# Retention, MoE and SOLU-MoE on one core: the attention of the later pairs in chunks of 64, with the products of two token blocks' h between the turns

## The chip, the cores and the metric

One core of one Trainium2 chip runs the whole program. The metric is the device time of one execution in microseconds (us), lower is better. The kernel before takes 635.72 us, the median of 3 runs (634.75 to 636.51).

## What is computed

```python
def _attn_ref(q, k, v):                     # 4 batches, 8 heads, 576 positions, head_dim 64
    scores = scale * np.matmul(q, k.transpose(0, 1, 3, 2))
    gamma = 1.0 - 2.0 ** (-5.0 - np.arange(H))
    Dmat = np.where(rel >= 0, gamma[:, None, None] ** rel[None, :, :], 0.0)   # rel = query - key position
    return np.matmul(scores * Dmat[None], v)

def _moe_ref(x, w_in, w_out):               # 2304 tokens, 512 -> 2048 -> 512
    h = x @ w_in
    g = h * np.clip(h + 3.0, 0.0, 6.0) / 6.0
    return g @ w_out

def _moe2_ref(x, w_in, w_out, g_ln):        # 512 -> 1024 -> 512
    h = x @ w_in                            # then softmax times h, layer norm, times g_ln
    return ln @ w_out

def reference(...):
    x = attention output, heads side by side: (2304, 512)
    return _moe2_ref(_moe_ref(x, ...), ...)
```

## The kernel before, in words

The 32 heads are worked off as 16 pairs (two heads of one batch, one in partitions 0 to 63, one in 64 to 127). The attention has no softmax, so it runs in chunks: inside a chunk of 128 positions the scores are formed, masked and multiplied with v; what came before the chunk enters through a 64x64 state of each head. The 576 positions are four chunks of 128 and one of 64. For a pair `pr` there are:

- `load_pair` (line 908): four loads from memory on SP's queue, k and q transposed (`rk`, `rq`), k as rows (`rn`), v (`rv`). It is called three pairs ahead.
- `prep` (929): v scaled by the decay, on ScalarE or VectorE.
- `scores` (946): products of k and q into `s0`, `s1`; ScalarE copies them to `st` with a scale, GpSimd's affine select sets the part above the diagonal to zero.
- `short` (970): the last chunk's scores `z`, VectorE's mask of them, and the products of the old pair with its states into `xp`.
- `chunk_states` (1005): k times v for each chunk into `u`; VectorE forms the four running states with five instructions.
- `values` (1047): v times the masked scores into `xp`; then `evac_x` (1059): VectorE multiplies by a table (`tab_sb`), ScalarE and VectorE or GpSimd split the result into a rounded part and a rest (`x`), or SP stores it (`xd`).

A product in full fp32 is two matmul instructions with a weight load each; 64x64 tiles are four corners of the array. The MoE products run as three products of rounded and rest parts.

The loop at line 1096 goes over the pairs. Turn `pr` has the scores of pair `pr`, the states of pair `pr`, and what remains of pair `pr - 1`. From turn 5 on (`A_FROM`) one half of an h (`h_of`, line 650: 6 matmuls of 128x128x512, for token block 0 and the first six column groups of w_in, `FIRST`) is put behind each turn: 12 halves in 12 turns. After the loop, block 0's second product (`x2_units(0, FIRST)`, accumulators `acc`) alternates with block 1's h (line 1207), then come block 4's h, block 1's second product, and from line 1231 the `paired` stage, whose seven products per step (`sa` to `sd`) need sums of tokens (`early_forms`, `x_sums`) and sums of weights (`in_pair`).

What sets the order: the matmuls run in the order of the program text. All other work is put in order by a planner (class `Plan`, line 110), which gives each operation a due time from the matmuls behind it, and lets some vector work go to VectorE or GpSimd (`either`). Buffers of a tag are handed on in program order. The pools `ps_a` (accumulators of the attention) and `pa` (its buffers) are released before `ps_c` (accumulators `acc`) and `pb` (buffers of the later stages, among them `ws`, `wbo`, `wbi`, `g2`) are opened: an operation on a buffer of `pb` waits for all users of `pa`.

The weights come as 64-bit words and are put together on the core: a load into `wraw`, two ScalarE instructions (`wz`, `wt`), two VectorE ones, then the split (`words_of`): ScalarE, and VectorE or GpSimd. `out_later` (534) does this for six further groups of w_out, through two buffers `ws`, and `in_pair(3)` follows them in the order of `wraw`.

Of the kernel before, what the change touches and what calls it, by code (L numbers as in the profile page):

```python
# [24 lines left out]
FA = 6  # L25
GAMMA = [1.0 - 2.0 ** (-5 - h) for h in range(H)]
N_DEC = H + H // 2 + H // 2 + H // 2
NPAIR = NH // 2
NV = 5
BLOCKS = [(0, 512), (512, 512), (1024, 512), (1536, 512), (2048, 256)]  # L30
# [7 lines left out]
EARLY = 3  # L38
NE = 4
# [314 lines left out]
def retention_hardswish_solu_kernel(ctx, tc, kt, qt, kn, vt, w1, w2i, w2o, gln, decay, place, out):  # L354
# [70 lines left out]
    tab_sb = [pa.tile([128, S], F32, name=f"tab_sb{p}") for p in range(NP)]  # L425
# [3 lines left out]
    HEADS, ALL = [slice(0, 64), slice(64, 128)], slice(0, 128)  # L429
    CHUNKS = [slice(128 * c, min(128 * c + 128, S)) for c in range(NV)]  # L430

# [9 lines left out]
    for h in range(2):  # L441
        ge.affine_select(
            out=mask4[HEADS[h]], in_=mask4[HEADS[h]], compare_op=ALU.is_ge, fill=0.0,
            base=0, pattern=[[0, NP], [1, 64]], channel_multiplier=-1,
        )
# [40 lines left out]
    def raw_of(src):  # L486
        b = buf("wraw", [128, 512, 2], "wraw", I32)
        move(512, lambda: sy.dma_start(out=b().rearrange("p n t -> p (n t)"), in_=src), (), (b,))
        return b
# [406 lines left out]
    PA = {"rk": 3, "rq": 4, "rn": 3, "rv": 3, "v": 3, "st0": 2, "st1": 2, "state": 2, "st4": 2, "xa": 2}  # L896
# [4 lines left out]
    def pbuf(tag, shape, name):  # L901
        return pl.buf((ps_a, tag, 1), shape, F32, name)

    def at_x(c):

        return slice(128 + CHUNKS[c].start, 128 + CHUNKS[c].stop)

    def load_pair(pr):

        if pr >= NPAIR:  # L910
            return
        early = pr < EARLY
        tag = "wi" if pr < 2 else "g"
        rk, rq, rn, rv = (
            buf("g" if i == 3 else tag, shape, f"raw{pr}_{i}") if early else abuf(name, shape, f"{name}{pr}")
            for i, (name, shape) in enumerate((
                ("rk", [128, S]), ("rq", [128, S + 128]), ("rn", [128, 512]), ("rv", [128, 9, D]),
            ))
        )
        move(288, lambda: sy.dma_start(out=rk(), in_=kt[pr]), (), (rk,))  # L920
        n = S if early else S + 128
        move(n / 2, lambda: sy.dma_start(out=rq()[:, :n], in_=qt[pr][:, :n]), (), ((rq, 0),))
        move(288, lambda: sy.dma_start(out=rv(), in_=vt[pr]), (), (rv,))
        move(256, lambda: sy.dma_start(out=rn(), in_=kn[pr]), (), (rn,))
        if early:
            move(64, lambda: sy.dma_start(out=rq()[:, n:], in_=qt[pr][:, n:]), (), ((rq, 1),))
        raws[pr] = rk, rq, rn, rv

    def prep(pr):

        if pr >= NPAIR:
            return
        rv = raws[pr][3]
        v = vs[pr] = abuf("v", [128, 9, D], f"v{pr}")
        p = pr % NP
        for i, (c0, n, at) in enumerate(((0, 4, 2 * p), (4, 4, 2 * p + 1), (8, 1, H + NP + p))):
            def go(e, c0=c0, n=n, at=at):
                o, i = (x()[:, c0:c0 + n].rearrange("p c d -> p (c d)") for x in (v, rv))
                if e is se:
                    se.activation(out=o, in_=i, func=ACTF.Copy, scale=decay_sb[:, at:at + 1])  # L940
                else:
                    ve.tensor_scalar(out=o, in0=i, scalar1=decay_sb[:, at:at + 1], scalar2=None, op0=ALU.mult)

            either(0.3 if n > 1 else 0.15, 0.5 if n > 1 else 0.33, go, (rv,), ((v, i),), "ACT").earliest = 5.6

    def scores(pr):

        sp = [pbuf(f"s{h}", [128, 512], f"s{pr}_{h}") for h in range(2)]
        st = sts[pr] = [abuf(f"st{h}", [128, 512], f"st{pr}_{h}") for h in range(2)]
        k, q, _, _ = raws[pr]  # L950

        def go():
            for c in range(4):
                for o in range(2):
                    for h in range(2):
                        te.matmul(
                            sp[h]()[HEADS[o], CHUNKS[c]], k()[HEADS[h], 128 * c + 64 * o:128 * c + 64 * o + 64],
                            q()[HEADS[h], CHUNKS[c]], start=(c == 0), stop=(c == 3),
                        )

        pl.op("PE", 0.92, go, (k, (q, 0)), sp)
        for h in range(2):
            on_act(0.6, lambda h=h: se.activation(
                out=st[h](), in_=sp[h](), func=ACTF.Copy, scale=GAMMA[2 * (pr % NP) + h] ** -128), (sp[h],), (st[h],))
            on_ge(0.66, lambda h=h: ge.affine_select(
                out=st[h](), in_=st[h](), compare_op=ALU.is_ge, fill=0.0,
                base=0, pattern=[[0, 4], [1, 128]], channel_multiplier=-1,
            ), (st[h],), (st[h],))

    def short(pr, now, old):  # L970


        reads, writes = [], []
        if now:
            zp = pbuf("z", [128, 64], f"z{pr}")
            st4 = sts4[pr] = abuf("st4", [128, 64], f"st4{pr}")
            k, q, _, _ = raws[pr]
            reads, writes = [k, (q, 0)], [zp]
        if old:
            xp = xps[pr - 1] = pbuf("xp", [128, 1024], f"xp{pr - 1}")  # L980
            oq, v, state, ost4 = raws.pop(pr - 1)[1], vs[pr - 1], states.pop(pr - 1), sts4.pop(pr - 1)
            reads, writes = [*reads, oq, v, state, ost4], [*writes, xp]

        def go():
            for h in range(2):
                if old:
                    te.matmul(xp()[HEADS[h], at_x(4)], v()[HEADS[1 - h], 8], ost4()[HEADS[1 - h]], start=True, stop=False)
                if now:
                    te.matmul(zp()[HEADS[h]], k()[HEADS[h], CHUNKS[4]], q()[HEADS[h], CHUNKS[4]], start=True, stop=True)
            if not old:  # L990
                return
            rq, st = oq(), state()
            for c, w, qc in (
                (1, st[:, 0], rq[:, CHUNKS[1]]), (3, st[:, 2], rq[:, S:]),
                (2, st[:, 1], rq[:, CHUNKS[2]]), (4, st[:, 3], rq[:, CHUNKS[4]]),
            ):
                for h in range(2):
                    r = HEADS[h if c < 3 else 1 - h]
                    te.matmul(xp()[HEADS[h], at_x(c)], w[r], qc[r], start=(c == 1), stop=False)

        pl.op("PE", 0.24 * now + (0.45 if now else 0.6) * old, go, reads, writes)
        if now:
            on_ve(0.25, lambda: ve.tensor_tensor(out=st4(), in0=zp(), in1=mask4[:, pr % NP], op=ALU.mult), (zp,), (st4,))

    def chunk_states(pr):

        rn, v = raws[pr][2], vs[pr]
        up = pbuf("u", [128, 4, 64], f"u{pr}")
        state = states[pr] = abuf("state", [128, 4, 64], f"state{pr}")

        def go():
            kn_ = rn().rearrange("p (c d) -> p c d", d=128)
            for c in range(4):
                for h in range(2):
                    o = HEADS[1 - h if c == 3 else h]
                    te.matmul(up()[o, c], kn_[:, c, HEADS[h]], v()[:, 4 * h + c], start=(c == 0), stop=(c == 3))

        pl.op("PE", 0.52, go, (rn, v), (up,))

        def sums():  # L1020
            ve.tensor_copy(out=state()[:, 0], in_=up()[:, 0])
            for c, to, at in (
                (1, ((ALL, ALL),), H + pr % NP), (2, tuple(zip(HEADS, HEADS[::-1])), H + pr % NP),
                (3, ((ALL, ALL),), H + 2 * NP + pr % NP),
            ):
                for i, o in to:
                    ve.scalar_tensor_tensor(
                        out=state()[o, c], in0=state()[i, c - 1], scalar=decay_sb[i, at:at + 1], in1=up()[i, c],
                        op0=ALU.mult, op1=ALU.add,
                    )  # L1030

        on_ve(1.45, sums, (up,), (state,))

    def places():

        pp = bank("place", at=0)
        row = buf("r", [128, NP, 128], "place_sb")
# [51 lines left out]
    for pr in range(EARLY):  # L1089
        load_pair(pr)  # L1090
# [5 lines left out]
    for pr in range(NPAIR + 1):  # L1096
        more, past, joined = pr < NPAIR, pr > 0, pr > A_FROM
        if more:
            scores(pr)
# [15 lines left out]
    for _ in hs:  # L1115
        pass
# [518 lines left out]
```

## Time and profile before

| | |
|---|---|
| median of 3 runs | 635.72 us |
| profiled execution: time | 635.21 us |
| profiled execution: span of the trace | 633.5 us |
| granted TensorE clock over the span | 1.00 |
| TensorE (PE) busy | 622.9 us, 98% |
| VectorE (DVE) busy | 467.3 us, 74% |
| ScalarE (ACT) busy | 398.2 us, 63% |
| GpSimd (POOL) busy | 306.6 us, 48% |
| DMA | 145.99 MB, mean 230 GB/s |

PE is the matmul side of TensorE and PEld its weight loads, which overlap. Matmuls are pipelined, so the length of one (0.22 to 0.27 us for the small ones) says little; what an instruction costs is the distance between the starts of neighbours. "issue" as the end of a wait means that nothing that the profile shows was waited for. "q8 instruction" is the DMA queue that brings TensorE's program.

### The profile page before, as it was taken

The numbers are of one execution on the slowest core, as the hardware profiler recorded it, in microseconds if no ns is written. First come the engines' busy times: TensorE is split into PE (matmuls) and PEld (weight loads), VectorE is DVE, ScalarE is ACT, GpSimd is POOL, SyncE is SP. The second block draws the span as 40 slices with busy tenths as digits, with TensorE's granted clock in tenths as the row PEclk, the third lists the DMA queues.
The fourth block names the chain that finished last, engine by engine and source line by source line (L and its number), as shares of the span: only waits on it lengthen the run. The fifth ranks groups of instructions, "written<-read, shape, count | busy, mean of one in ns | idle before, by whom it ended". The sixth has DMA issues, their size and how long they took to land.

```text
span 633.5 us, 11326 instructions
## 1 busy us (share of the span) xinstructions
PE 622.9 (98%) x4095; PEld 519.3 (82%) x4095; DVE 467.3 (74%) x835; ACT 398.2 (63%) x687; POOL 306.6 (48%) x307
## 2 busy tenths in 40 slices
PE   7999999999999999999999999999999999999997
PEld 5788778889788888887888888888888888888887
DVE  4878899986778776789587787543687877878750
ACT  4778776874766561468476665421587777787582
POOL 6545553203144321533145230632379899999453
PEclk9999999999999999999999999999999999999999
DMA  9999997679756686645997669975585544344451
GB/s 326 381 347 380 398 328 255 252 233 310 242 190 230 224 301 242 228 161 192 360 345 271 223 224 386 391 255 187 153 237 116 114 90 113 101 84 101 83 106 61
DMA packets 92347, 145.99 MB, mean 230 GB/s; under 512 B 43906, under 2 KB 50178, under 8 KB 92292
## 3 DMA queue, kind: packets, MB, share of 16 engines
q1 hardware_dynamic: 92144, 145.26, 69.6%
q8 instruction: 32, 0.52, 0.3%
q14 instruction: 23, 0.19, 0.1%
q10 hardware_dynamic: 148, 0.02, 0.0%
HBM read 92.56 MB, written 43.25 MB: 214 GB/s over the span
## 4 chain that ended last, share of the span: by engine, by line
PE 81%; DMA 10%; DVE 5%; ACT 1%; issue 1%; SPq 1%; POOL 0%; DVEq 0%; POOLq 0%; ACTq 0%
PE acc L67 26%; PE h L67 20%; PE o L67 16%; PE sd L67 4%; PE sa L67 4%; PE sc L67 4%; DMA xd<-xa 4%; PE x L67 2%; PE sb L67 2%; PE xp L67 2%; DMA w1f_a<-w1w 2%; DMA w2s<-ws 1%; DMA wraw<-wf 1%; PE s L67 1%; DVE ws L67 1%
## 5 line engine op out<-in xcount | busy, mean ns | idle before, releaser
L67 PE MATMUL acc<-g,w1l 128*128 128x512 f32 x624 | 154.1, 389 | 0.0
L67 PEld LDWEIGHTS acc<-g,w1l 128*128 128x128 f32 x624 | 117.1, 188 | 24.4
L67 PE MATMUL o<-w,lt 128*128 128x512 f32 (+1 forms) x456 | 103.0, 378 | 0.0
L67 PEld LDWEIGHTS o<-w,lt 128*128 128x128 f32 x456 | 82.4, 188 | 16.3 <-POOL lt L67 0.4
L67 POOL TENSOR_TENSOR lt<-lT,lt 128x512 fp32r<-128x512 f32 x36 | 61.6, 1730 | 15.3 <-ACT lt L67 15.3
L67 ACT ACTIVATE e<-h,stat 128x1024 f32<-128x1024 f32 x36 | 41.3, 1148 | 35.7 <-DVE stat L67 35.4
L67 PE MATMUL h<-w2t,xt 128*128 128x512 f32 x216 | 53.5, 389 | 0.0
L67 PEld LDWEIGHTS h<-w2t,xt 128*128 128x128 f32 x216 | 40.3, 188 | 8.2
L67 PE MATMUL h<-x,w 128*128 128x512 f32 (+1 forms) x216 | 45.9, 361 | 0.0
L67 PE MATMUL acc<-g,w 128*128 128x512 f32 (+1 forms) x216 | 44.2, 355 | 1.4 <-DVE xa L67 0.9
L67 POOL TENSOR_TENSOR w1f_s<-ws,w1f_s 128x512 fp32r<-128x512 f32 x13 | 17.8, 1368 | 54.5 <-ACT w1f_s L67 54.5
L67 PEld LDWEIGHTS acc<-g,w 128*128 128x128 f32 x216 | 36.4, 189 | 8.5 <-ACT g L67 1.3
L67 PEld LDWEIGHTS h<-x,w 128*128 128x128 f32 x216 | 34.9, 189 | 7.1 <-issue 1.9
L67 PE MATMUL h<-w2b,xt 128*128 128x512 f32 x162 | 39.8, 390 | 0.0
L67 ACT ACTIVATE wz<-wraw 128x512 f32<-128x512 f32 x44 | 29.2, 669 | 14.2 <-DMA wraw<-in_w2o_dram 5.6
L67 DVE CUSTOM_DVE_ANT_0 wz<-wz,wt 128x1024 uint16<-128x1024 uint16 x44 | 36.1, 826 | 1.6 <-ACT wt L67 0.3
L67 ACT ACTIVATE wt<-wraw 128x512 int32<-128x512 uint32 x48 | 31.9, 665 | 8.2 <-DMA wraw<-in_w2o_dram 7.0
L67 DVE SCALAR_TENSOR_TENSOR h<-h,e 128x1024 f32<-128x1024 f32 x18 | 32.3, 1796 | 5.4 <-ACT e L67 5.3
L67 DVE TENSOR_SCALAR e<-h,stat 128x1024 f32<-128x1024 f32 x18 | 20.6, 1143 | 20.1 <-POOL stat L67 20.1
L67 PEld LDWEIGHTS h<-w2b,xt 128*128 128x128 f32 x162 | 30.2, 188 | 6.1
L67 DVE CUSTOM_DVE_ANT_0 h<-h,h 128x512 f32<-128x512 f32 x36 | 24.6, 683 | 12.9 <-ACT h L67 6.3
L67 POOL TENSOR_TENSOR xt<-x2r,xt 128x512 fp32r<-128x512 f32 (+1 forms) x18 | 23.9, 1346 | 19.2 <-ACT xt L67 19.2
(194 smaller groups left out, 1358.7 us busy)
## 6 DMA issues: line engine op xcount, KB each, us to landing
w1l<-w1s SPq DMA_DIRECT2D x34, 512.0 KB, 5.9
wraw<-in_w_dram SPq DMA_DIRECT2D x32, 512.0 KB, 5.9
w1s<-w1o SPq DMA_DIRECT2D x10, 512.0 KB, 3.3
x2l<-x2s SPq DMA_DIRECT2D x18, 256.0 KB, 6.7
x2f<-x2o SPq DMA_DIRECT2D x18, 256.0 KB, 3.9
x2r<-x2f SPq DMA_DIRECT2D x9, 512.0 KB, 4.3
rq<-in_qt_dram SPq DMA_DIRECT2D x13, 352.0 KB, 6.2
out_dram<-osb SPq DMA_DIRECT2D x17, 256.0 KB, 2.0
```

What stands on the lines that cost most here:

```text
L67: return lambda *args, **kw: self.keep(op(*args, **kw))
```

## The change

Pairs 0 to 4 (`LONG = 5`) stay in chunks of 128; their scores are now 64 rows by 128 columns of the array, half as many instructions, and the extra copy of q (`rqx`) is a load of its own. From pair 5 on the 576 positions are nine chunks of 64, every product is a 64x64 tile with 64 columns, and `attend(pr)` puts the products of pair `pr` (scores `s`, chunk products `u`) and of pair `pr - 1` (states `f`, values `y`) side by side, so that the four corners of the array work on four of them: 17 rounds of four products. VectorE now masks the scores straight from PSUM (`masked`), forms seven states with five instructions (ScalarE copies the first part), and multiplies by the table in two parts; the affine select is gone for these pairs.

The halves of h behind the turns are now those of block 0 and of block 1, 24 in all, handed out by a budget of 3.4 us per turn. Block 1's g lies in a tag of the pool `pa`. After the loop come block 1's second product, block 4's h, and block 0's second product, each without anything between.

```diff
+L, NC, C0 = 64, S // 64, 5
+LONG = 5
+FILL = 3.4
     def split_of(t, ff, name, src, r, tag="g", n=512):
-        w = GK[t, ff] = buf(tag, [128, 2, n], name, F32R)
+        w = GK[t, ff] = buf(tag, [128, 2, n], name, F32R) if tag else pl.buf((pa, "g", FA), WIDE, F32R, name)
     def h_of(t, ff, tag="g", extra=0.0):
-        hp = bank(f"h{t}_{ff}", n, None if t else 0)
+        hp = bank(f"h{t}_{ff}", n, None if t > 1 else 0)
-    PA = {"rk": 3, "rq": 4, "rn": 3, "rv": 3, "v": 3, "st0": 2, "st1": 2, "state": 2, "st4": 2, "xa": 2}
+    PA = {"rk": 3, "rq": 3, "rqx": 3, "rn": 3, "rv": 3, "v": 3, "st0": 2, "st1": 2, "state": 2, "xa": 3}
+    PARTS = (slice(0, C0), slice(C0, NC))
     # prep, from pair LONG on: one instruction over all nine chunks
+                either(0.42, 0.9, go, (rv,), ((v, i),))
+    def masked(pr, i, sp):
+        on_ve(0.1 + 0.067 * n, lambda: ve.scalar_tensor_tensor(
+            out=st(), in0=sp()[:, :n * L].rearrange("p (c q) -> p c q", q=L), scalar=decay_sb[:, at:at + 1],
+            in1=causal.unsqueeze(1).to_broadcast([128, n, L]), op0=ALU.mult, op1=ALU.mult), (sp,), (st,))
+    def state_of(pr, up):
+        on_act(0.4, lambda: se.activation(out=of(state())[:, 0], in_=us()[:, 0], func=ACTF.Copy), (up,), (state,))
+        def sums():
+            add(r[:, 1], r[:, 0], one, x[:, 1])
+            for c in range(1, 4):
+                add(r[:, 1, c], r[:, 1, c - 1], two, r[:, 1, c])
+            add(r[:, 0, 1:], r[:, 1, :3], one, x[:, 0, 1:])
+        on_ve(1.35, sums, (up, state), (state,))
+    def attend(pr):
+        now, old = pr if pr < NPAIR else None, pr - 1 if pr > LONG else None
...
+        def mm(b, c, left, right, swap, last=False):
+            for h in range(2):
+                o = HEADS[1 - h if swap else h]
+                te.matmul(b()[o, SHORT[c]], left(HEADS[h]), right(HEADS[h]), start=(b, h) not in begun, stop=last)
...
+        run([[(u, c), (y, c)] for c in range(5)], ...)
+        run([[(u, c), (f, c - 4)] for c in (5, 6, 7)], ...)
+            state_of(now, up)
+        run([[(s, 0), (f, 4)]], ...)
+            evac_x(old, 0, xp[0], xa)
+        run([[(s, c), (f, c + 4)] for c in (1, 2, 3, 4)], ...)
+            masked(now, 0, sp[0])
+        run([[(s, c), (y, c)] for c in (5, 6, 7, 8)], ...)
+            masked(now, 1, sp[1])
+            evac_x(old, 1, xp[1], xa)
+            split_x(old, xa)
+    def fillers():
+        for t, tag in ((0, "g"), (1, None)):
+            for ff in FIRST:
+                for i, _ in enumerate(h_of(t, ff, tag)):
+                    if i < 2:
+                        yield 1.36
     for pr in range(NPAIR + 1):
...
+        if pr < LONG:
+            long_scores(pr)
+            load_pair(pr + EARLY)
+            long_sums(pr)
+            prep(pr + 1)
+            long_rest(pr, pr - 1 if pr else None)
+        else:
+            if pr == LONG:
+                long_rest(None, pr - 1)
+            load_pair(pr + EARLY)
+            attend(pr)
+            prep(pr + 1)
         if pr >= A_FROM:
-            next(hs, None)
+            spent -= FILL
+            while spent < 0:
+                spent += next(fill, 9.0)
-    for i, _ in enumerate(x2_units(0, FIRST, evac_partial, ends=1)):
-        if i % NP == NP - 1:
-            for _ in h_of(1, FIRST[i // NP]):
-                pass
+    for _ in x2_units(1, FIRST, evac_partial):
+        pass
     for ff in FIRST:
         for _ in h_of(4, ff, next(slots_4)):
             pass
-    for _ in x2_units(1, FIRST, evac_partial):
+    for _ in x2_units(0, FIRST, evac_partial):
         pass
```

## Rows read from the trace of the kernel before

**Rows 1.** First part of the page and the clock line (engines; granted clock in tenths).

```profile
PE 622.9 (98%) x4095; PEld 519.3 (82%) x4095; DVE 467.3 (74%) x835; ACT 398.2 (63%) x687; POOL 306.6 (48%) x307
...
PEclk9999999999999999999999999999999999999999
```

**Rows 2.** Waits of PE, first 110 us: who, for whom; us, times, longest.

```profile
PE xp L67 <- issue: 2.3, 2, 1.4
...
PE acc L67 <- DVE xa L67: 0.9, 1, 0.9
```

**Rows 3.** Timeline of PE, one turn: start us, length us, instructions, form, count.

```profile
31.46 1.10 PE L67 MATMUL s<-rq,rk 64*64 64x128 f32 x32
32.38 0.22 PE L67 MATMUL z<-rq,rk 64*64 64x64 f32 x1
...
32.49 0.62 PE L67 MATMUL xp<-rq,state 64*64 64x128 f32 x16
33.04 0.69 PE L67 MATMUL u<-v,rn 128*64 128x64 f32 x16
33.56 1.05 PE L67 MATMUL xp<-st,v 128*64 128x128 f32 x16
34.53 1.65 PE L67 MATMUL h<-x,w 128*128 128x512 f32 x6
36.12 0.34 PE L67 MATMUL s<-rq,rk 64*64 64x128 f32 x4
```

**Rows 4.** Busy time by stretch: length; each engine's us (instructions); clock; DMA share, GB/s.

```profile
24.45:82.37 57.92, 55.71 (x1079) 44.62 (x1077) 46.45 (x115) 45.53 (x95) 33.41 (x38) 1.00 1.01 375
82.37:115.00 32.63, 32.62 (x142) 26.59 (x143) 30.96 (x41) 22.56 (x40) 13.78 (x8) 1.00 0.84 277
115.00:140.47 25.47, 25.47 (x147) 22.53 (x147) 22.52 (x46) 20.85 (x42) 1.98 (x2) 1.00 0.72 230
```

**Rows 5.** The same view between two stops of PE, and one later stretch.

```profile
15.82:21.52 5.70, 5.54 (x128) 4.68 (x128) 3.74 (x9) 3.50 (x10) 3.40 (x6) 1.00 1.05 393
...
34.53:41.50 6.97, 6.97 (x127) 5.54 (x129) 6.03 (x18) 5.68 (x13) 2.75 (x5) 1.00 0.99 334
```

**Rows 6.** Timeline of PE at two stops; in brackets the wait before.

```profile
15.82 0.33 PE L67 MATMUL xp<-raw,state 64*64 64x64 f32 x3 [1.38 <-issue]
...
28.25 0.65 PE L67 MATMUL xp<-rq,state 64*64 64x128 f32 x16 [0.90 <-issue]
```

**Rows 7.** DMA queues in 25.7-25.8, 29.9-30.1, 36.3-36.45 us: packets, MB, share.

```profile
q8 instruction: 1, 0.02, 69.2%
...
q8 instruction: 1, 0.02, 38.9%
...
q8 instruction: 1, 0.02, 45.8%
```

**Rows 8.** Groups of VectorE and GpSimd, 31.46 to 78.20 us: busy, mean ns.

```profile
L67 DVE TENSOR_TENSOR xa<-xp,tab_sb 128x576 f32<-128x576 f32 x10 | 7.5, 753 | 1.0 <-PE h L67 1.0
...
L67 DVE SCALAR_TENSOR_TENSOR state<-state,decay_sb,u 128x64 f32<-128x64 f32 x20 | 5.6, 281 | 0.7
...
L67 POOL TENSOR_SCALAR_AFFINE_SELECT st<-st 128x512 f32<-128x512 f32 x20 | 12.6, 654 | 17.4 <-ACT st L67 17.4
```

**Rows 9.** Groups of VectorE, 82.37 to 143 us.

```profile
L67 DVE TENSOR_TENSOR x_t<-xs_b,x_t 128x512 fp32r<-128x512 f32 x4 | 2.6, 677 | 0.0
...
L67 DVE SCALAR_TENSOR_TENSOR gf<-r,h 128x256 f32<-128x256 f32 x6 | 2.4, 412 | 0.1
...
L67 DVE TENSOR_TENSOR xs_b<-xs_b,xs_b 128x1024 f32<-128x1024 f32 x1 | 1.2, 1219 | 0.0
```

**Rows 10.** SP's issue of the second w_in load; GpSimd's last step on it.

```profile
22.08 0.33 SPq L67 DMA_DIRECT2D wraw<-in_w_dram  x1
...
34.53 1.31 POOL L67 TENSOR_TENSOR w<-wz,w 128x512 fp32r<-128x512 f32 x1
```

**Rows 11.** Timeline of PE: the first product after the attention.

```profile
82.37 3.01 PE L67 MATMUL acc<-g,w 128*128 128x512 f32 x12 [0.88 <-DVE xa L67]
```

More of the change, by code (lines that the diff above doesn't have):

```diff
@@ L353, in retention_hardswish_solu_kernel @@
 @with_exitstack
-def retention_hardswish_solu_kernel(ctx, tc, kt, qt, kn, vt, w1, w2i, w2o, gln, decay, place, out):
+def retention_hardswish_solu_kernel(ctx, tc, kt, qt, qx, kn, vt, w1, w2i, w2o, gln, decay, place, out):
     nc = tc.nc
@@ L429, in retention_hardswish_solu_kernel @@
     HEADS, ALL = [slice(0, 64), slice(64, 128)], slice(0, 128)
+    SHORT = [slice(L * c, L * c + L) for c in range(NC)]
     CHUNKS = [slice(128 * c, min(128 * c + 128, S)) for c in range(NV)]
@@ L939, in go @@
                 if e is se:
-                    se.activation(out=o, in_=i, func=ACTF.Copy, scale=decay_sb[:, at:at + 1])
+                    se.activation(out=v()[:, cs], in_=rv()[:, cs], func=ACTF.Copy, scale=decay_sb[:, at:at + 1])
                 else:
[L942 to L1032, printed above, removed]
+                    e.tensor_scalar(
+                        out=v()[:, cs], in0=rv()[:, cs], scalar1=decay_sb[:, at:at + 1], scalar2=None, op0=ALU.mult)
@@ new lines, in long_sums, with go @@
+    def long_sums(pr):
+        rn, v = raws[pr]["rn"], vs[pr]
+        up = pbuf("u", f"u{pr}")
+        state = states[pr] = abuf("state", [128, 4, 64], f"state{pr}")
+        def go():
+            for c in range(4):
+                for h in range(2):
+                    o = HEADS[1 - h if c == 3 else h]
+                    te.matmul(up()[o, SHORT[c]], rn()[:, 128 * c + 64 * h:128 * c + 64 * h + 64],
+                              v()[:, SHORT[4 * h + c]], start=(c == 0), stop=(c == 3))
+        pl.op("PE", 0.6, go, (rn, v), (up,))
+        def sums():
+            u = up()[:, :4 * D].rearrange("p (c d) -> p c d", d=D)
+            ve.tensor_copy(out=state()[:, 0], in_=u[:, 0])
+            for c, to, at in (
+                (1, ((ALL, ALL),), H + pr % NP), (2, tuple(zip(HEADS, HEADS[::-1])), H + pr % NP),
+                (3, ((ALL, ALL),), H + 2 * NP + pr % NP),
+            ):
+                for i, o in to:
+                    ve.scalar_tensor_tensor(
+                        out=state()[o, c], in0=state()[i, c - 1], scalar=decay_sb[i, at:at + 1], in1=u[i, c],
+                        op0=ALU.mult, op1=ALU.add,
+                    )
+        on_ve(1.45, sums, (up,), (state,))
@@ new lines, in long_rest, with at_x, go, values @@
+    def long_rest(pr, past):
+        reads, writes = [], []
+        more = pr is not None
+        if more:
+            zp = pbuf("acc", f"z{pr}")
+            st4 = sts4[pr] = abuf("st1", [128, 64], f"st4{pr}")
+            k, q = raws[pr]["rk"], raws[pr]["rq"]
+            reads, writes = [k, q], [zp]
+        if past is not None:
+            xp = [pbuf(f"x{i}", f"xp{i}_{past}") for i in range(2)]
+            old, v, state, ost4 = raws.pop(past), vs[past], states.pop(past), sts4.pop(past)
+            oq, ox = old["rq"], old["rqx"]
+            reads, writes = [*reads, oq, ox, v, state, ost4], [*writes, *xp]
+        def at_x(c):
+            i, at = divmod(c, 3)
+            return xp[i]()[:, 128 * at:128 * at + (128 if c < 4 else 64)]
+        def go():
+            for h in range(2):
+                if past is not None:
+                    te.matmul(at_x(4)[HEADS[h]], v()[HEADS[1 - h], SHORT[8]], ost4()[HEADS[1 - h]], start=True, stop=False)
+                if more:
+                    te.matmul(zp()[HEADS[h], :64], k()[HEADS[h], CHUNKS[4]], q()[HEADS[h], CHUNKS[4]], start=True, stop=True)
+            if past is None:
+                return
+            rq, st = oq(), state()
+            for c, w, qc in (
+                (1, st[:, 0], rq[:, CHUNKS[1]]), (3, st[:, 2], ox()),
+                (2, st[:, 1], rq[:, CHUNKS[2]]), (4, st[:, 3], rq[:, CHUNKS[4]]),
+            ):
+                for h in range(2):
+                    r = HEADS[h if c < 3 else 1 - h]
+                    te.matmul(at_x(c)[HEADS[h]], w[r], qc[r], start=(c == 1), stop=False)
+        pl.op("PE", 0.24 * more + (0.45 if more else 0.6) * (past is not None), go, reads, writes)
+        if more:
+            on_ve(0.25, lambda: ve.tensor_tensor(out=st4(), in0=zp()[:, :64], in1=mask4[:, pr % NP], op=ALU.mult), (zp,), (st4,))
+        if past is None:
+            return
+        v, st = vs.pop(past), sts.pop(past)
+        def values():
+            for c in range(4):
+                for h in range(2):
+                    te.matmul(at_x(c)[HEADS[h]], v()[:, SHORT[4 * h + c]], st()[:, h, CHUNKS[c]], start=False, stop=(c in (2, 3)))
+        pl.op("PE", 1.0, values, (v, st), xp)
+        xa, p = abuf("xa", [128, S], f"xa{past}"), past % NP
+        table(lambda: xa()[:, :384], lambda: xp[0]()[:, :384], p, 3, 128, (xp[0],), ((xa, 0),))
+        table(lambda: xa()[:, 384:512], lambda: xp[1]()[:, :128], p, 1, 128, (xp[1],), ((xa, 1),))
+        table(lambda: xa()[:, 512:], lambda: xp[1]()[:, 128:192], p, 1, 64, (xp[1],), ((xa, 2),))
+        split_x(past, xa)
@@ L1081, in idle_mm, with evac_x @@
+    def evac_x(pr, i, xp, xa):
+        cs = PARTS[i]
+        n = cs.stop - cs.start
+        table(lambda: xa()[:, cs.start * L:cs.stop * L], lambda: xp()[:, :n * L], pr % NP, n, L, (xp,), ((xa, i),))
     def idle_mm(n, warm=[]):
```

220 lines of the change are left out of this document (143 added, 77 removed).

## The prediction

> **What bounds the kernel now.** I read the page's first part, then PE's waits, then its timeline turn by turn, and last the stretches by engine. TensorE is busy 98% of the span at full granted clock [rows 1], and in the first 110 us it waits for little: 2.3 us of "issue" in two stops and 0.9 us for the last `xa` [rows 2]. From 28.25 us on it stands still only before the first `acc`. So a microsecond of matmul taken out is a microsecond of time, unless a new wait takes its place. The reader should see the turn: scores from 31.46, `z` and `xp` from 32.38, `u` from 33.04, `values` from 33.56, half an h from 34.53, next scores at 36.12 [rows 3]: 4.66 us, of which 3.07 are attention and 1.59 the six matmuls of h. In the packed stretch behind the attention 144 matmuls of 512 columns (two of them not recorded) take 32.63 us, 0.227 each [rows 4], so six are 1.36 us; the remaining 0.23 is the change between small tiles and the whole array.
>
> **What the change does to TensorE.** Eight matmuls of 64 columns on the four corners start within 32.38 to 32.49 [rows 3]; I take 0.115 us for such a round. One `attend` is 17 rounds: 17 x 0.115 = 1.96 us. Twelve `attend`s (pair 5 alone, ten mixed, pair 15 alone; a half-filled round lasts as long) are 23.5 us. Eleven changes of tile with their way back I put at 0.33 each, 0.23 from the h and 0.1 for the way into it: 3.6 us. The 24 halves of h are 24 x 1.36 = 32.6. Pair 4's rest costs 1.6 us (its 16 `values` matmuls are the 0.97 from 33.56 to 34.53 [rows 3], the `xp` ones some 0.6), and 0.5 us of waiting for its states, which now have one pair's products less in front of them. Sum: 61.8 us. Before, the same work is the stretch 24.45 to 82.37, 57.9 us with its waits, and block 1's twelve halves behind it, 16.3 us: 74.2 [rows 4]. **Gain: 12.4 us**, if nothing new is waited for. The order of the second products is only turned round, and their matmuls stay.
>
> **The end of the attention costs 3.3 us.** A budget of 3.4 us per turn hands out 3, 2, 3, 2, ... halves, so the 24 are gone in turn 14, and turns 15 and 16 have nothing behind them. VectorE's part of a turn, by column from the `xa` row (753 ns for 576 columns) and by the 281 ns of a 64-column state [rows 8]: states 3 x 0.28 + 2 x 0.35 = 1.5, masks 0.8, tables 0.8. In turn 15 `u` is done after 0.9 us; a ScalarE copy (0.4, an estimate), the states, the first table and the first mask follow one another to about 4.0 us, and turn 16 needs that mask for its first round at 2.0. That is a wait of 2.0; 0.4 for the same reason before turn 15; and 0.9 for the last tables before the accumulators open, as today [rows 11], which the gain above had taken out.
>
> **TensorE's program has to be fetched, and faster: 4.5 us.** The two longest stops, 1.38 and 0.90 us, are of "issue" [rows 6], one of them between the instructions of one product, so no data is missing there. Between the end of one such stop and the end of the next TensorE ran 128 matmuls and 128 weight loads [rows 5]: 256 instructions. The packet of 16 KB on the instruction queue that precedes the stop's end starts at about 25.77 [rows 7], and work goes on at 28.25: 2.5 us later. Following blocks begin at 28.25 and 34.53 and their packets start at 30.03 and 36.37 [rows 7], so a block is there some 1.8 + 2.5 = 4.3 us after the one before it begins (6.7 us for the block from 21.52). Today a block lasts 5.7 to 7.0 us [rows 5], and that is just enough. In the new turns 272 instructions run in 1.96 us and 24 or 36 in the h: about 300 per 5.0 or 6.4 us. A block with two or three halves of h inside it lasts 4.7 to 6.0 us; one that holds a part of them only, 3.0 to 3.5. Counting instructions from the start, I find four of the short kind among the eleven before the last turns: 4 x (4.3 - 3.2) = 4.4, and 0.1 for the spread of the others. The bounds are 1 us, if the loads, now 1.12 MB per longer turn rather than 1.18, leave the queue freer, and 9 us, if it takes 5.3 us each time. The Trainium skill, "Runtime: NRT & Kernel Launch", section "Instruction fetch mechanics", has the same block of 256 instructions, but calls its crossing mostly hidden; the size agrees with the trace, the hiding does not [rows 6]. By that page this term would be nothing.
>
> **The other engines.** The affine select (654 ns, two per pair [rows 8]) and two ScalarE copies go, off the path. VectorE gets 3.1 us per pair for about 2.4 now (`xa` 0.75, five state instructions of 0.28 or 0.22, `z` 0.22 [rows 8]). It is busy 46 of 58 us there [rows 4]; a turn is longer by more than a microsecond, so I cost this at nothing in the middle; without that cover it would be 0.7 per turn. w_in's words are needed sooner, one group in 4.6 us instead of 9.3: the second is used at 31.3 us, while today its load is issued at 22.08 and GpSimd ends at 35.8 [rows 10]. SP's queue has to put it before loads of pairs, which saturate the DMA there (393 GB/s [rows 5]). Between nothing and 4 us; I take 0.7, since the planner orders loads by due time and pair 7 is needed later than now. SP's load of q is 64 KB shorter for late pairs, and pairs 0 to 4 have the same bytes in five loads.
>
> **Forecast:** 635.2 (the profiled execution: 633.5 of span and 1.7 around it; the median of the runs is 0.5 above) - 12.4 + 3.3 + 4.5 + 0.7 = **631.3 us**.
>
> **Rivals.**
>
> *VectorE becomes the bound behind the attention (slower).* Block 1's g lies in `pa`, so `pb` opens only after block 1's second product, about 16 us behind the attention, where it now opens at 82. All of `out_later`, `early_forms` and block 4's splits waits for it, and VectorE, busy 31 of 32.6 us there today [rows 4], idles and then has it all at once: six `out_later` 8.5 us (two half done before), block 4's gates and splits 12 x 0.4 = 4.7, sixteen sums and splits x 0.68 and four differences x 1.22 = 15.7 [rows 9], `in_pair(3)` 6.4, the first gates of `paired` 3.4: 38.7 us, in the 25.5 us that the two steps before `paired` take (115.00 to 140.47 [rows 4]) and five steps of `paired` more, until the last form is used: 5 x (6 x 0.227 + 9 x 0.127, the short matmuls from the same row) = 12.5, 38.0 in all. GpSimd can take some. At the 95% that VectorE reaches today from 82.37 to 115 [rows 4] it would be late by 2.7 us, at the 88% of the stretch after [rows 4] by 6.0, and with the chain of stores through two `ws` on top I put it at 7.5: 631.3 + 7.5 = 638.8. It decides from 4.4 us of such waits on, when 635.7 is reached. For it: `in_pair(3)` comes behind `out_later` in the order of `wraw`. Against: due times spread the 38.7 us, and some is done by GpSimd. Chance 0.22.
>
> *The fetch is hidden.* Longer turns relieve the DMA queues, and packets start earlier: 631.3 - 3.5 = 627.8. Chance 0.18.
>
> *w_in's words come late.* The full 4 us instead of 0.7: 634.6. Chance 0.12.
>
> *The corners don't keep the pace.* The round of 0.115 us is read from eight matmuls in a row; the longest mixed run is 24 from 32.38 to 33.04, 27 ns each with its change of tile [rows 3]. At 25 ns, 136 matmuls take 3.4 us, 1.44 more per turn, 17 in all, and the fetch is hidden then: 631.3 + 17.3 - 4.5 = 644. The rows speak against it, as 14 ns stand in them. The Trainium skill, "TensorE: Matmul & The Clock Gate", section "Back-to-back issue gap", gives about 25 ns as the floor for up to 64 columns; the eight matmuls here are below it. Chance 0.08.
>
> **How the numbers follow.** The forecast's own case (629 to 634) has 0.40. About 0.3% (1.9 us) is what a measurement of this kernel can tell from no change. Faster by more: 0.34 of the first case, 0.18, 0.04 of the late words, 0.02 of VectorE's: 0.58. Within it: 0.05, 0.08, 0.06: 0.19. Slower: 0.01 and 0.14 and 0.08: 0.23. For eight in ten I leave out the slow corners, the far half of VectorE's case and a fetch of nothing with no wait at all: 626 to 639.
>
> **What would show it.** Right: rounds of eight matmuls 0.11 to 0.12 us apart; a turn of about 5.0 and 6.4 us; "issue" waits 256 instructions apart, most of them between small tiles; 2 to 3 us of waits in turn 16 for a VectorE mask; the second product of block 1 beginning near 95 us and `paired` near 136 instead of 140.47. Wrong: waits of `sa` to `sd` for VectorE sums or splits (the first rival), a waiting h in turns 5 to 9 for a split of w_in (the third), a pitch of 20 ns and more (the fourth), or an accumulator that waits for anything in the middle of a turn, which I have at nothing.

## The result, and the profile after

The new kernel takes 641.81 us in the median (641.00 to 643.57) against 635.24 us for the kernel before on the same chip: ratio 1.0115, 95% interval 1.0095 to 1.0134. It is about 1% slower; 631.3 us had been forecast, in a range of 626 to 639. The profiled execution took 643.57 us, with a span of 641.8.

First part of the page of the new kernel, its clock line and the row of the instruction queue (they answer to [rows 1]):

```profile
PE 622.6 (97%) x4543; PEld 517.9 (81%) x4543; DVE 477.5 (74%) x855; ACT 381.6 (59%) x649; POOL 315.7 (49%) x297
...
PEclk9989979999999999999999999999999999999999
...
q8 instruction: 36, 0.59, 0.4%
```

TensorE is busy as long as before with 448 more matmuls, and its clock line has two dents, which the line of before has not. Where it waits from 24 to 110 us (who, for whom; us, times, longest; [rows 2]):

```profile
PE s L70 <- issue: 3.5, 1, 3.5
PE h L70 <- issue: 3.4, 2, 2.6
PE xp L70 <- DVE xa L70: 1.6, 1, 1.6
PE xp L70 <- DVE state L70: 1.1, 1, 1.1
PE u L70 <- ACT r L70: 1.0, 1, 1.0
PE acc L70 <- DVE xa L70: 0.7, 1, 0.7
PE xp L70 <- issue: 0.6, 2, 0.3
PE xp L70 <- DVE st L70: 0.4, 2, 0.2
PE h L70 <- POOL w L70: 0.4, 1, 0.4
```

Busy time by stretch, columns as in [rows 4]: from the end of pair 4's own products to the first `acc`, from there to `paired`, and two pieces inside the first stretch:

```profile
24.45:106.37 81.92, 70.11 (x1676) 56.73 (x1677) 70.73 (x146) 42.14 (x80) 50.94 (x38) 0.94 0.89 315
106.37:148.62 42.25, 42.25 (x216) 35.74 (x217) 28.75 (x46) 23.82 (x46) 7.21 (x4) 1.00 0.60 196
40.50:43.50 3.00, 3.00 (x15) 1.89 (x17) 1.48 (x3) 1.15 (x2) 1.14 (x1) 0.50 0.85 321
82.50:87.50 5.00, 5.00 (x19) 3.82 (x15) 3.67 (x5) 0.00 (x0) 3.13 (x2) 0.50 0.76 254
```

The first stretch holds the same work as the 74.2 us of before [rows 4] and lasts 81.9 us; forecast were 70.3. From `paired` to the end it is 493.2 us, before 493.0. So the loss lies in the attention: waits of "issue", 7.5 us in five stops, and two pieces at a granted clock of 0.50, 1.2 GHz. The three largest stops in the timeline of PE (in brackets the wait; [rows 6]):

```profile
39.73 3.61 PE L70 MATMUL h<-x,w 128*128 128x512 f32 x9 [2.55 <-issue]
...
74.91 0.50 PE L70 MATMUL h<-x,w 128*128 128x512 f32 x1 [0.87 <-issue]
...
82.01 0.37 PE L70 MATMUL s<-rq,rk 64*64 64x64 f32 x2 [3.53 <-issue]
```

Each comes in the middle of one product. Counting recorded TensorE instructions (matmuls, weight loads and the semaphore instructions between them) in order of their start, all five stops stand at 449 + 256k instructions, k whole; in before, those at 15.82, 21.52 and 28.25 us do too. A block below is such a piece of 256 instructions. The packet of the instruction queue starts 2.3 to 2.5 us ahead of each resumption; here the rows of the queue for 37.2 to 37.3 and 79.5 to 79.65 us, ahead of the two longest stops:

```profile
q8 instruction: 1, 0.02, 64.9%
...
q8 instruction: 1, 0.02, 36.6%
```

Ahead of that lies the time between the beginning of a block and the packet for the next: 1.2 to 3.5 us for the turns of before from 28.25 us on and 3.3 to 4.3 at its three stops; 0.8 to 4.7 here (mean 2.8, blocks that begin from 24 to 100 us). With the 2.3 to 2.5 us a block arrives up to 7.1 us after the one ahead begins, where the prediction had 4.3.

### The profile page after: what moved, and what is told of

Same layout as the page of the kernel before. It is cut to its first block, busy times and chain, and to the rows that moved or that the text cites. A ratio compares the mean times of both kernels' runs of the same rounds, so it can differ in the third digit from the quotient of the medians.

```text
span 641.8 us, 12160 instructions
## 1 busy us (share of the span) xinstructions
PE 622.6 (97%) x4543; PEld 517.9 (81%) x4543; DVE 477.5 (74%) x855; ACT 381.6 (59%) x649; POOL 315.7 (49%) x297
## 4 chain that ended last, share of the span: by engine, by line
PE 87%; DVE 5%; DMA 4%; issue 2%; ACT 1%; POOL 0%; SPq 0%; ACTq 0%
PE acc L70 25%; PE h L70 21%; PE o L70 15%; PE sc L70 6%; PE sd L70 6%; PE sa L70 5%; PE sb L70 3%; PE x L70 2%; PE xp L70 2%; DVE wz L70 1%; PE u L70 1%; DMA w1s<-w1o 1%; DMA rv<-in_vt_dram 1%; PE s L70 1%; DMA raw_rn<-in_kn_dram 1%
## 5 line engine op out<-in xcount | busy, mean ns | idle before, releaser
L70 PE MATMUL h<-x,w 128*128 128x512 f32 (+1 forms) x216 | 49.1, 382 | 3.8 <-issue 3.4
L70 PEld LDWEIGHTS h<-x,w 128*128 128x128 f32 x216 | 37.2, 199 | 11.6 <-issue 4.1
L70 ACT ACTIVATE g<-gf 128x512 fp32r<-128x512 f32 (+1 forms) x44 | 26.0, 596 | 13.6 <-DVE gf L70 13.5
```

What stands on the lines that cost most here:

```text
L70: return lambda *args, **kw: self.keep(op(*args, **kw))
```

## The experiments

**e1: long chunks for all pairs, in the new order.** The edit:

```diff
-LONG = 5
+LONG = 16
```

> All 16 pairs stay in chunks of 128 (the boundary moved from pair 5 to pair 16); the 24 halves of h behind the turns, block 1's g in the pool pa and the order of the second products stay as in the change. Theory F (TensorE's program: 256 instructions are used up sooner than the next block arrives, and a stop of about 3 us is followed by some microseconds at half clock): a turn has some 174 instructions in 6.5 us, so no stop of 'issue' over 1 us after the first 30 us and a granted clock of 1.00: 635 to 637 us. Rival V (the late opening of pb, behind block 1's second product, makes VectorE late): that part is unchanged, so the loss stays: 639 us or more.

Measured: 640.96 us, ratio 1.0099 (1.0078 to 1.0120). No stop of issue and no half clock; an attention of 3.45 us a turn against 3.07 before (the new order changes the tile's shape once more), 11 times: 4.2 us. The time is the one that rival V had given, but of the 5.8 us of span above before only 1.9 lie behind the first `acc`. In PE's waits from 24 to 110 us:

```profile
PE acc L70 <- DVE xa L70: 1.1, 1, 1.1
PE xp L70 <- DVE xa L70: 0.9, 1, 0.9
PE xp L70 <- DVE x L70: 0.8, 1, 0.8
```

The stops belong to the 64-chunks, not to the order of the second products. But the kernel without them is no faster, so it can't serve as their price.

**e2: 64-chunks, h and second products in the order of before.** One half of h per turn, of block 0 only; then block 0's second product with h of block 1 between, block 1's last:

```diff
-FILL = 3.4
+FILL = 1.36
-        for t, tag in ((0, "g"), (1, None)):
+        for t, tag in ((0, "g"),):
...
-    for _ in x2_units(1, FIRST, evac_partial):
-        pass
+    for i, _ in enumerate(x2_units(0, FIRST, evac_partial, ends=1)):
+        if i % NP == NP - 1:
+            for _ in h_of(1, FIRST[i // NP]):
+                pass
...
```

> The attention in chunks of 64 stays, but h goes back: one half of block 0 behind each turn, block 1's h between block 0's second products, pa free at the end of the attention. Theory F: a turn has about 284 instructions in 3.7 us of matmuls, a block takes 4.3 to 6.7 us to arrive, so nearly every turn stops for 1 to 3 us: 'issue' waits of 12 to 25 us in all, stretches at half clock, 640 to 650 us. Rival V: pb opens early again and the gain of the shorter products shows: 627 to 630 us.

Measured: 648.65 us, 1.0223 (1.0184 to 1.0261). Stops of issue fall to 4.4 us, where 12 to 25 were expected, and with one half of h per turn the data are late (`u` for DVE `state` 3.9, h for ACT `x` 3.8, `u` for POOL `v` 2.5), and three pieces run at half clock. The change needs its filling; leaving it out is worse. So the number falls in the fetch theory's range, but not for its reason alone.

**e3: halves of h spread inside the turn.** `attend` calls `one`, which issues a half of h, at two places in its middle:

```diff
+        between()
...
+        between()
...
-            attend(pr)
+            attend(pr, one)
```

> The change with the same matmuls, but one half of h put into the middle of attend twice per turn (behind the states' rounds and behind the first mask) and the rest behind the turn, so that 256 instructions never lie in one burst. Two more changes of tile per turn cost about 0.38 us each, 7 us in ten turns. Theory F: 'issue' waits fall from 9 us to 2 to 4 us and the half-clock stretches (4.3 us) go: 637 to 640 us. Rival V or any rival without the fetch: only the changes of tile are seen, 648 to 650 us.

Measured: 646.19 us, 1.0194 (1.0160 to 1.0228). Stops of issue fall from 7.5 to 3.8 us, as they should if blocks that hold only small products are the short ones; one piece of half clock stays (44.5 to 47.9 us). Two more changes of tile per turn, some 0.38 each, and data waits take more than that back. The time lies between the two that were expected.

**e4: no loads from pair 8 on.** Pairs 8 to 15 read the buffers of pairs 5 to 7:

```diff
+        if pr >= LONG + 3:
+            raws[pr] = raws[pr - 3]
+            return
```

> The change, but pairs 8 to 15 use the data of pairs 5 to 7 again and load nothing: 9 MB of loads are left out, so the output of those pairs is another. Theory F with the DMA queue as the cause of the delay: instruction packets start within 1.5 us of the block's first instruction instead of 1.3 to 4.7, 'issue' waits fall below 3 us, no half clock: 631 to 635 us. If the delay does not come from the load on the DMA queues: the waits stay at 7 us or more, 640 to 642 us.

Measured: 644.86 us, 1.0162 (1.0119 to 1.0205). For the blocks that begin from 41 to 75 us packets start 0.6 to 2.1 us after their block, and the first `acc` comes at 101.27 instead of 106.37. But stops of issue are 6.5 us, where less than 3 were expected: one of 4.2 us, the longest of all runs, ends at 41.09 us, behind a stretch in which the queues still move 314 GB/s, with half clock behind it, and one of 2.1 at 79.77. What is gained is given back later: PE waits 4.6 us for `x2p`. The last of these waits, in PE's timeline:

```profile
166.88 0.39 PE L70 MATMUL acc<-g,w 128*128 128x256 f32 x1 [2.48 <-ACT x2p L70]
```

and the stretch just behind it, by engine:

```profile
168.00:171.50 3.50, 3.50 (x10) 2.73 (x10) 0.91 (x2) 2.65 (x7) 0.00 (x0) 0.54 0.81 246
```

**e5: the kernel before with more instructions, nothing else.** From pair 5 on, scores and `values` in two pieces of 64 columns (the `values` are shown):

```diff
-                for h in range(2):
-                    te.matmul(xp()[HEADS[h], at_x(c)], v()[:, 4 * h + c], st[h]()[:, CHUNKS[c]], start=False, stop=(c in (2, 3)))
+                for part in cut(c, pr):
+                    for h in range(2):
+                        te.matmul(
+                            xp()[HEADS[h], 128 + part.start:128 + part.stop], v()[:, 4 * h + c], st[h]()[:, part],
+                            start=False, stop=(c in (2, 3) and part.stop == 128 * c + 128),
+                        )
```

> The kernel before, with one thing changed: from pair 5 on its scores' and values' products are cut from 128 columns to 64, so that the same columns, the same arithmetic and the same data take about 96 more TensorE instructions per turn (some 284 with the half of h, against 188), and a block of 256 instructions lasts about 4.2 us instead of 6.2. Fetch theory (TensorE stops because the next block of its program has not come): stops of issue at nearly each of the some eleven block edges between 24 and 82 us, 0.5 to 3 us each, 6 to 12 us in sum, the granted clock at half for a few us if one of them exceeds 2.5 us: 641 to 648. Rival (number of instructions plays no part; the new kernel's stops come from its order and data): the same matmul columns in smaller pieces cost at most 1 us: 635 to 636.5, no stops of issue but the two that were there.

Measured: 650.37 us, 1.0239 (1.0198 to 1.0281). PE's waits from 24 to 110 us are these alone:

```profile
PE s L67 <- issue: 4.2, 4, 2.4
PE xp L67 <- issue: 3.1, 2, 2.3
PE z L67 <- issue: 1.7, 1, 1.7
PE h L67 <- issue: 1.4, 1, 1.4
```

The stretch up to the first `acc`, and a piece of it behind the stop of 2.42 us:

```profile
24.45:96.51 72.06, 61.68 (x1615) 50.70 (x1610) 45.05 (x117) 45.70 (x95) 33.16 (x39) 0.95 0.90 315
29.00:31.50 2.50, 2.50 (x42) 2.25 (x44) 1.33 (x5) 2.50 (x7) 2.01 (x3) 0.50 0.72 261
```

The stretch that took 57.92 us [rows 4] takes 72.06. Of the 14.1 us 9.5 are stops of issue (10.4 less the 0.9 that was there), 3.4 are the half clock behind two of them (half of 6.8 us) and 1.3 the smaller products (3.20 against 3.08 us of attention, 11 times); before's 0.9 us for the last `xa` is not there, so these parts are good to about 1 us. Order, data and loads are those of before. The number of instructions alone makes the stops, and they are twice the 4.5 us that the forecast gave the new kernel.

**e6: halves of h for the last two turns.** The 24 halves handed out as 3,2,3,2,3,2,2,2,1,1,2,1:

```diff
-            spent -= FILL
-            while spent < 0:
-                spent += next(fill, 9.0)
+            for _ in range({5: 3, 6: 2, 7: 3, 8: 2, 9: 3, 10: 2, 11: 2, 12: 2, 13: 1, 14: 1, 15: 2, 16: 1}[pr]):
+                next(fill, None)
```

> The new kernel with the same 24 halves of h handed out otherwise: 3,2,3,2,3,2,2,2,1,1,2,1 over turns 5 to 16, so that the last two turns have h behind them too. Ledger theory: the end of the attention (4.0 us of waits and empty work in the new kernel's turns 15 and 16) falls to about 1.3, and the instruction stops move but stay about as long in sum (9 us with the half clock behind them 13): 639, 637 to 641. Fetch theory in its strong form (turns with a single half of h behind them are the shortest, 240 instructions in 3.7 us, so the stops grow there by what the tail gives): 641 to 643. Rival (VectorE's work decides the end of the attention whatever lies behind the turns): waits of the tail stay at 3.5 to 4: 641 to 642, without longer issue stops.

Measured: 648.32 us, 1.0200 (1.0171 to 1.0229), above every expectation. The attention did shorten: `acc` begins at 104.22, 2.2 us earlier, with stops of issue of 6.6 us. But `paired` to the end lasts 498.3 us instead of 493.2; in it `sc` waits 2.4 us for ACT `g`, with 3.4 us of half clock at its end.

**e7: 64-chunks for the last six pairs only.** The long pairs' products stand in the order of before, their scores are 64x64 tiles again, and the halves of h are handed out as follows:

```diff
-LONG = 5
+LONG = 10
...
+            for _ in range({5: 1, 6: 1, 7: 1, 8: 1, 9: 1, 10: 3, 11: 3, 12: 3, 13: 3, 14: 3, 15: 3, 16: 1}[pr]):
```

> Pairs 0 to 9 as long chunks with more than one tile shape, 10 to 15 in chunks of 64, the long ones with their scores as 64x64 tiles and u last, one half of h behind each of turns 5 to 9 and 16, three behind each of 10 to 15. Three halves behind every short turn give 308 instructions in 6.6 us, a block of 256 in some 5.5 us; so fewer instructions per us than in the new kernel. Fetch theory: issue stops of 1 to 3 us in sum, no half clock; six short turns save some 6 x 0.8, and the tail is about 1.5: 633, 630 to 636. Rival (the gain of the short chunks is lost wherever they stand, by VectorE's waits behind the attention, as block 1 still comes before block 0's second product): 637 to 641, with accumulators that wait for VectorE after 100 us.

Measured: 642.74 us, 1.0112 (1.0087 to 1.0137). One stop of issue (2.4 us) with half clock behind it, so of the fetch theory's expectation the sum of the stops holds, the full clock does not. The time doesn't either: behind `paired` (143.15 us) come 2.8 us of waits of `sb` for forms of w1 and half clock again.

**e8: no loads of pairs from pair 6 on.** The products are those of the new kernel, on data of pairs 3 to 5:

```diff
+        if pr > LONG:
+            raws[pr] = dict(raws[pr - 3])
+            return
```

> The new kernel, in which pairs 6 to 15 read the inputs of pairs 3 to 5 that lie in the chip already, so that no load of a pair is issued from pair 6 on; the instructions of TensorE are unchanged (the output of those pairs is that of other data; this is what is left out). Fetch theory with the queues' load as its cause: the packets of the instruction queue start within 1 to 2 us after a block is begun, issue stops sum to less than 2.5 us instead of 9.5 to 11, the granted clock stays at 1.0 through the attention, and block 1's second product begins by 98 us instead of 106.4. The time: 634 to 637 if all of that is kept, up to 640 where the accumulators then wait for VectorE (x2p, gf), which would show the first rival of the prediction as next in line. Rival (the fetch takes its 4 to 6 us whatever the loads do): stops of issue 8 us and more, block 1's second product after 103 us, 640 to 642.

Measured: 635.28 us against 634.71, 1.0004 (0.9985 to 1.0022). PE's longest waits from 24 to 110 us:

```profile
PE xp L70 <- issue: 2.0, 1, 2.0
PE h L70 <- issue: 1.3, 1, 1.3
PE u L70 <- DVE state L70: 1.3, 1, 1.3
```

The stretches up to the first `acc` and on to `paired`:

```profile
24.45:97.50 73.05, 65.61 (x1677) 53.50 (x1677) 71.24 (x143) 40.94 (x79) 51.03 (x38) 1.00 0.60 196
97.50:139.50 42.00, 42.00 (x216) 35.79 (x217) 28.68 (x46) 23.86 (x46) 7.21 (x4) 1.00 0.59 192
```

With 196 GB/s instead of 315, packets start 2.0 us after their block begins in the mean, stops of issue are 3.3 us (less than 2.5 were expected), the clock stays full and `acc` comes 8.9 us earlier: 4.2 of that are stops, and the new kernel's half clock cost some 4.3 (see below). So the loads lengthen a block's way, and the stops with the clock account for the loss. Packets still start up to 3.5 us late here: the pairs' loads are a part of the delay, not all of it. Nor do bytes alone set it: before, with 375 GB/s [rows 4], has a mean of 2.4. And the kernel is then no faster than before.

**e9 and e10: the place of a block's edge.** Short chunks for pairs 11 to 15; e10 differs from e9 only in two halves of h, in turn 11 instead of 16. Against e7, with e9's halves and then e10's:

```diff
-LONG = 10
+LONG = 11
...
+            for _ in range({5: 1, 6: 1, 7: 1, 8: 1, 9: 1, 10: 2, 11: 1, 12: 3, 13: 3, 14: 3, 15: 4, 16: 3}[pr]):
...
+            for _ in range({5: 1, 6: 1, 7: 1, 8: 1, 9: 1, 10: 2, 11: 3, 12: 3, 13: 3, 14: 3, 15: 4, 16: 1}[pr]):
```

> Pairs 0 to 10 as long chunks (scores as 64x64 tiles, u last), 11 to 15 in chunks of 64, halves of h 1,1,1,1,1,2,1,3,3,3,4,3 over turns 5 to 16. Counted in e7's trace, a turn of 64-chunks with three halves is 310 TensorE instructions (272 of attention in 2.1 us, 38 of h in 4.3), so the edge of a 256-block moves on by 54 each turn; counted so, turns 12 to 15 begin at about 50, 104, 158 and 212 instructions into a block, and every block there holds the whole of a turn's h and lasts 5.6 to 6.0 us. Fetch theory: no stop of issue above 0.8 us in turns 11 to 15 and no half clock there; 634, 632 to 637. Rival (short chunks stop wherever they stand, from data or order): waits of 2 us and more in these turns, 638 or more.

> The kernel of e9 with two halves of h moved from turn 16 to turn 11, and nothing else: turns 12 to 15 then begin at about 76, 130, 184 and 238 instructions into a block, so that the block that begins at turn 15's start holds little but the 64-chunk products and lasts some 2.1 us. Fetch theory: one stop of issue of 2 to 3.5 us at the end of turn 15's attention, half clock for some 3.5 us behind it if it exceeds 2.2, together 4 to 5 us more than e9: 638 to 640. Rival (the place of the edges plays no part): within 1 us of e9.

Measured: e9 642.05 us (1.0096, 1.0063 to 1.0129), e10 643.41 us (1.0128, 1.0084 to 1.0172). The stops of issue in turns 11 to 15 in PE's timeline, two in e9:

```profile
82.39 0.27 PE L70 MATMUL xp<-st,v 64*64 64x64 f32 x2 [0.29 <-issue]
87.65 0.39 PE L70 MATMUL h<-x,w 128*128 128x512 f32 x1 [0.57 <-issue]
```

one in e10:

```profile
88.89 0.21 PE L70 MATMUL xp<-st,v 64*64 64x64 f32 x1 [2.89 <-issue]
```

and e10's stretch behind it, by engine, at half clock:

```profile
89.50:92.50 3.00, 3.00 (x9) 2.32 (x8) 1.70 (x6) 0.81 (x2) 0.10 (x1) 0.50 1.02 380
```

Where the edges were put decides whether the stop comes, at the place and of the size that counting gave. Their times don't follow: e9 begins `acc` at 97.35 us, e10 at 99.94 (2.6 later, where 4 to 5 were expected), yet their spans are 640.9 and 640.1. In e9 TensorE waits behind that as follows (97 us to the end), with 3.4 us of half clock at the end of the first and 3.4 more behind the one of 1.7:

```profile
PE sc L70 <- ACT g L70: 2.7, 1, 2.7
PE acc L70 <- DMA w1l<-w1s: 2.1, 2, 1.7
PE sa L70 <- POOL w1f_a L70: 1.0, 1, 1.0
PE acc L70 <- ACT x2p L70: 0.7, 1, 0.7
```

VectorE's longest wait in e9 from 95 to 155 us:

```profile
DVE xs_b L70 <- PE acc L70: 13.6, 1, 13.6
```

**e11: the loads of the late pairs in two halves each.**

```diff
-            move(n / 2, lambda r=r, src=src: sy.dma_start(out=r(), in_=src[pr]), (), (r,))
+            for a in (slice(0, n // 2), slice(n // 2, n)) if pr >= LONG else (slice(0, n),):
+                move((a.stop - a.start) / 2, lambda r=r, src=src, a=a: sy.dma_start(out=r()[:, a], in_=src[pr][:, a]), (),
+                     ((r, a.start),) if pr >= LONG else (r,))
```

> The new kernel with every load of a pair from pair 5 on cut into two loads of half the columns, the same bytes in twice as many transfers of half the size. Theory A (a packet of the instruction queue waits for the large pieces that lie in front of it): packets start earlier after a block's begin, 1.5 us in the mean instead of 2.6, issue stops fall from 9.5 to below 5 us: 634 to 638. Theory B (it is the bytes in flight that count): within 1.5 us of the new kernel, 640 to 643. Theory C (more transfers on SyncE's queue come late): waits for rv, rn, rk or rq loads, above 643.

Measured: 656.02 us, 1.0312 (1.0277 to 1.0348). Packets start 3.5 us after their block begins in the mean, once 8.8; the stops of issue are 9.5 us, and converted words and `v` come late too (`h` for ACT `w` 2.2, `u` for POOL `v` 2.3). Smaller transfers make it worse; theories A and B fall, and C's number is met, though not by the loads that it named.

## Why the prediction was wrong

**What held.** The rounds: 17 rounds of eight last 2.0 us (34.06 to 36.05 us, 0.117 a round; forecast 0.115), so the rival of slow corners falls. The Trainium skill, "TensorE: Matmul & The Clock Gate", section "Back-to-back issue gap", has about 25 ns as the floor from one matmul to the next at up to 64 columns; 15 ns are measured. A turn with two halves is 5.09 us and with three 6.45, forecast 5.01 and 6.37. The words of w_in cost 0.4 us. The end of the attention costs 4.0 us for 3.3, but by other waits, so that the nearness is luck: of the 2.0 us for a VectorE mask in turn 16 there are 0.2, and instead `u` waits 1.0 for ScalarE's `r` and `xp` 1.1 for the states.

**The step that failed is the fetch, and what hangs on it.** The prediction took 4.3 us for a block's arrival from two packets of before [rows 7], which started 1.8 us after their blocks. Eight packets of those turns start 1.2 to 3.5 us after, and the 6.7 us for the block from 21.52, which the prediction names itself, was the better guide. At the five stops it was 5.5 to 7.1 us: 7.5 us of stops instead of 4.5, inside the stated bound of 9. The count was off the other way: where the prediction had four short blocks, the trace has two, with 2.9 and 3.6 us of work, and they make 6.1 of the 7.5 us. The Trainium skill, "Runtime: NRT & Kernel Launch", section "Instruction fetch mechanics", calls the crossing mostly hidden; e5 shows 9.5 us more stops from the number of instructions alone.

**The clock had no term.** At the stops of 2.55 and 3.53 us the granted clock is 0.50 from 40.2 to 43.6 and, beginning within the stop, from 81.2 to 88.0 us. By the same work at full clock (nine matmuls of h in 3.53 us for 2.27, the products up to 45.73 in 2.1 for 1.75; the products from 82.01 to 88.06 in 6.05 for the 3.35 of e8 from 75.61) that is 1.6 + 2.7 = 4.3 us. Before had no stop that long [rows 6], so its trace didn't show it, but the prediction should have asked what a longer stop does.

**The sum again**, for the stretch from 24.45 us: 70.3 forecast, 81.9 measured. Stops 3.0 above, clock 4.3, the wait of turn 5 for `xa` 0.2 above (0.7 of its 1.6 us lie behind 24.45, for 0.5), the end of the attention 0.7 above, the words 0.3 below. Of the remaining 3.7, 0.9 are the 0.08 in each of eleven turns, and 1.1 are a wait in the middle, which the prediction had at nothing: in the turns that begin at 50.53, 56.16, 62.90 and 68.17 us the first `xp` products wait for VectorE's mask `st` of the turn before. So the attention of these turns lasts 2.3 to 2.7 us instead of 2.14, stops left out. The first of them, in the timelines of VectorE and PE:

```profile
50.49 0.54 DVE L70 SCALAR_TENSOR_TENSOR st<-s,decay_sb,causal 128x320 f32<-128x320 f32 x1
...
51.08 0.27 PE L70 MATMUL xp<-st,v 64*64 64x64 f32 x2 [0.22 <-DVE st L70]
```

The last 1.7 us I have not separated. Behind the stretch come 0.5 us up to `paired` and 0.2 after: 631.3 + 11.6 + 0.7 = 643.6.

**VectorE's rival** did not decide: the new kernel lost 0.7 us there. But it stands right behind, as kernels with the new order show (start of the first `acc`, of `paired`, and from there to the end, us; one profiled execution each):

| kernel | first `acc` | `paired` | to the end |
|---|---|---|---|
| before | (98.7 with block 1's h) | 140.5 | 493.0 |
| after | 106.4 | 148.6 | 493.2 |
| e8 | 97.5 | 139.5 | 493.9 |
| e3 | 107.6 | 152.6 | 492.1 |
| e1 | 102.6 | 144.9 | 494.4 |
| e4 | 101.3 | 145.7 | 496.1 |
| e11 | 113.4 | 156.7 | 497.6 |
| e7 | 101.2 | 143.2 | 497.7 |
| e6 | 104.2 | 147.0 | 498.3 |
| e10 | 99.9 | 141.8 | 498.3 |
| e9 | 97.4 | 140.2 | 500.7 |

Those of 496 us and more have a piece of half clock of 3.4 us behind `paired` (e9 two), those of 492 to 494 none. In e9 the rival's mechanism is to be seen. VectorE idles 13.6 us for block 1's product, as it said; then it works without a gap from 140.65 to 149.07 us, and it reaches `gf`, which the late `g` needs, at 148.41, 4.9 us after ScalarE's `r` for it is done (the stretch ahead of that, columns as in [rows 4]):

```profile
140.65:148.41 7.76, 5.01 (x30) 4.08 (x28) 7.76 (x8) 6.48 (x15) 6.70 (x6) 1.00 0.91 336
```

From `paired` on e9 takes 7.7 us more than before. That this is near the 7.5 us at which the prediction priced the rival is chance: the waits of 2.7, 2.1 and 1.0 and half of the 6.8 us of half clock are 9.2, before has 1.6 of waits there, and the 2.1 are for loads of w1l at 224 to 227 us. VectorE idles 12.4 us in the new kernel too, without such waits after; why that one and e8 are spared and e9 is not, no run settles. In e8 the forecast's own mechanism is nearly undisturbed and it still takes 635.3, not 631.3: its stops are 1.2 us below the term, but turn 5, the attention's end (4.3) and the pace of the turns are 3.9 above, and 1.1 lies behind.

None of these kernels beats the one before, and e8, with loads left out, only equals it.

## What to carry to other kernels

Cutting products into smaller tiles saves columns but multiplies instructions: count TensorE's instructions per microsecond in every stretch of 256, not in the mean, and compare with the latest arrival of a block that the trace shows under the same DMA load, not with a typical one. Price a stop with the slow clock that may follow it. When an early stretch gets shorter, look at what the next stage waits for before booking the gain.

## What the hardware did that I had not expected

**Half clock behind short stops of any cause.** Most stops of 2.2 us and more had 3.4 to 6.8 us at 1.2 GHz behind them or from their last part on: for the program (2.55 and 3.53; e4 4.20; e5 2.42 and 2.27; e6 2.25 and 2.60; e7 2.35; e10 2.89) and for data (e4 2.48 for `x2p`, e6 2.45 and e9 2.66 for `g`). The length alone does not decide. A stop of 2.85 us in e11 was followed by full clock, and the next half clock there begins at 61.35 us (PE's timeline, and the stretch behind the stop):

```profile
45.32 0.27 PE L70 MATMUL xp<-st,v 64*64 64x64 f32 x2 [2.85 <-issue]
...
45.32:49.32 4.00, 4.00 (x35) 3.35 (x35) 3.89 (x8) 2.92 (x5) 3.89 (x3) 1.00 0.74 233
```

Nor had the stops of 2.04 us in e8, 2.05 and 2.12 in e4 or 1.38 in before half clock behind them, while one of 1.66 in e9 (to 227.12 us, for w1l) had it, from 227.2 to 230.6. In e2 and e3 it also fell behind groups of shorter waits.

**The next block is asked for late.** In the fast turns the packet for a block starts only after the block ahead has begun, 0.8 to 4.7 us after in the new kernel; behind 120 us, where nearly every block lasts over 20 us, it starts between 4.7 us before that and 0.6 after.

**More, smaller transfers delay it.** The mean delay rose from 2.8 us to 3.5 in e11, with the same bytes in twice as many loads, and fell to 2.0 in e8, without loads of pairs.
